# Two fp32 expert layers by seven products: block results finished inside PSUM, second products summed by DMA, units interleaved

## The chip, the cores and the metric

The kernel runs on one core of a Trainium2 chip. The time is that of one execution on the device in microseconds, from the first to the last instruction and the little around it. The engines are called PE (TensorE, the matmuls), PEld (its weight loads), DVE (VectorE), ACT (ScalarE), POOL (GpSimd) and SP (SyncE, which only starts transfers).

## The reference

```python
q_bits = (einsum('bhsd,dk->bhsk', q, proj) > 0)            # q, k, v: (2, 8, 768, 64); proj: (64, 6)
mask = q_bucket[:, :, :, None] == k_bucket[:, :, None, :]  # buckets: the six bits as a number
scores = where(mask, q @ k.T / sqrt(64), -1e9)
attn = exp(scores - max); attn = attn / (sum + 1e-9)
x = (attn @ v), heads side by side                         # (1536, 512)
h = x @ w_in; g = h - tanh(h); x = g @ w_out               # d_ff 2048
g = x @ w_gate; silu = g / (1 + exp(-g))                   # d_ff 1536
out = (silu * (x @ w_val)) @ w_out2                        # (1536, 512)
```

All of it is float32. The weights of the two expert layers arrive as 64-bit floating point numbers and are converted to float32 on the chip.

## The kernel before, in words

**Attention** runs first: 8 pairs of heads, 12 steps each (`declare_step`, L599), about 2.4 us a step. It ends near 257 us. Its transposes use both halves of the PSUM tile `t`, its second matmul the bank `x`, its hash bits the bank `h`.

**The expert layers** follow. The first product of a layer (with `w_in`, or with `w_gate` and `w_val`) is cut into units: one weight, one block of 256 columns (`i`), one block of 768 tokens (`sb`, two of them). A unit is computed as a 2 x 2 block product by seven products in place of eight (`PRODUCTS`, L736): sums and differences of the four blocks of x (made once for each token block by `x_blocks`, L332) times sums and differences of the four blocks of the weight (`declare_in`, L252). Every factor is held as a high and a low part, whose difference keeps float32's precision, so a product is two k steps of three terms: six matmuls of 128x128 by 128x384 (L769). In `products` (L741) the seven results gather in three PSUM banks: two of an `s` tile and one of `x` or `h`, by turns. Partial results are copied to SBUF on the way (`snap`, L753, ACT) and added to later ones (`add`, L756, DVE, result in SBUF). Each of the four finished 128 x 384 blocks of a unit goes through an activation: tanh on ACT and a subtraction (L721, L722), sigmoid and a multiplication (L727, L728), or the multiplication with the gate's result (L733). Then `split_g` makes its high part on ACT (L708) and its low part on POOL (L709).

**The second products** (`out_group`, L800) are groups of six matmuls (L820): 8 groups of 384 columns for a unit of layer 1, 6 of 512 columns for a pair of gate and value units. A group writes one of the two halves of `t`, and its result is added to an accumulator in SBUF by DVE (L836; for the first column block a copy by ACT or DVE, L833 and L834). At the end SP stores the accumulators in 12 transfers (L840). There are 16 units in layer 1 and 24 in layer 2, and in each the groups of an earlier unit are placed after given products (`share`, L885).

**Weights** come in chunks of 512 KB by SP (L229) and are converted by three DVE instructions (`convert`, L231, L234, L237); `declare_in` forms the block differences (L261, L264, L266) and `split_w` the parts (L243 on ACT, L245 on POOL). `declare_out` does it for the second weights (L277, L279).

**The order** of all instructions is worked out before the program is written: every operation is declared with the engines that may run it, an estimated time on each, what it reads and writes and a due time (`Plan.op`, L79); `Plan.order` (L99) plays this through, and at each moment a free engine takes the ready operation with the earliest due time. The program then issues each engine's instructions in that order. Operations marked `late` wait until attention is through, since the accumulators, the second weights and part of x's factors take over its room in SBUF (L908 to L912).

## Time and profile before

| | |
|---|---|
| median of 3 runs | 882.77 us (880.28 to 884.28) |
| the profiled execution | 878.98 us |
| its span, first to last instruction | 877.0 us |
| mean granted TensorE clock | 0.994 of full speed |

The time of the profiled execution stands for its span and 2 us around it. Busy times are read against the span; an instruction's duration is the bar that the profile draws, and the bars of successive matmuls overlap. The line numbers are those of the code above.

### The profile page before, as it was taken

Reading aid. Unit: us, or ns where it says so; the run is one execution under the profiler, and the core shown is the slowest. Engines: PE = TensorE matmul, PEld = TensorE weight load, DVE = VectorE, ACT = ScalarE, POOL = GpSimd, SP = SyncE. Lnnn points to the kernel's source line nnn. Section 1 sums busy time; section 2 is a strip of 40 time slices with the busy share of each in tenths; the row PEclk is TensorE's granted clock in tenths of the full one; section 3 lists DMA queues with packets and bytes.
Section 4 is the critical chain, followed back from the end, with each engine's and each line's share of the span. In section 5 each row is a group of like instructions: output and inputs, shape, how many; then the busy total and the mean of one; then the engine's idle time right before and its main releaser. Section 6 shows DMA issues by size and latency. Waiting matters only on the chain.

```text
span 877.0 us, 12166 instructions
## 1 busy us (share of the span) xinstructions
PE 789.9 (90%) x4332; PEld 660.4 (75%) x4332; DVE 639.1 (73%) x987; ACT 424.0 (48%) x804; POOL 529.6 (60%) x497
## 2 busy tenths in 40 slices
PE   5999999999996888988999898989989899999995
PEld 3666666666665867888889787877878888788883
DVE  6887777777858853766867779897876987877452
ACT  4787778766744533333433354444433334334220
POOL 4665677544857644665865678478585865848130
PEclk9999999999998999999999999999999999999999
DMA  8644554542111120221121210112212221210002
GB/s 214 163 121 126 128 119 116 134 89 76 55 67 49 49 72 25 73 72 49 49 88 57 72 59 14 48 38 84 96 49 85 67 89 49 72 50 23 1 37 108
DMA packets 25659, 66.46 MB, mean 76 GB/s; under 512 B 3936, under 2 KB 9312, under 8 KB 25600
## 3 DMA queue, kind: packets, MB, share of 16 engines
q1 hardware_dynamic: 25088, 64.76, 24.8%
q10 hardware_dynamic: 464, 0.80, 0.4%
q8 instruction: 34, 0.56, 0.3%
q0 software_dynamic: 48, 0.13, 0.1%
q14 instruction: 25, 0.20, 0.1%
HBM read 46.03 MB, written 3.15 MB: 56 GB/s over the span
## 4 chain that ended last, share of the span: by engine, by line
PE 68%; DVE 21%; ACT 4%; issue 3%; POOL 2%; DMA 1%; DVEq 0%; ACTq 0%
PE t L820 24%; PE s L769 20%; PE x L664 8%; PE t L640 7%; PE s L611 6%; DVE acc L836 6%; DVE m L620 2%; DVE f L234 2%; PE h L769 2%; DVE ct L756 2%; DVE acc L324 1%; ACT ct L622 1%; PE x L769 1%; DVE f L231 1%; ACT acc L833 1%
## 5 line engine op out<-in xcount | busy, mean ns | idle before, releaser
L769 PE MATMUL s<-x,wi 128*128 128x384 f32 x1200 | 241.1, 341 | 12.6 <-ACT ct L753 6.5
L769 PEld LDWEIGHTS s<-x,wi 128*128 128x128 f32 x1200 | 209.6, 188 | 28.7 <-ACT ct L753 13.7
L820 PE MATMUL t<-op,wo 128*128 128x384 f32 x768 | 157.1, 344 | 30.3 <-DVE acc L836 22.7
L820 PEld LDWEIGHTS t<-op,wo 128*128 128x128 f32 x768 | 132.6, 189 | 46.8 <-DVE acc L836 36.3
L709 POOL TENSOR_TENSOR op<-ct,op 128x384 fp32r<-128x384 f32 x112 | 125.7, 1132 | 65.3 <-ACT op L708 59.5
L836 DVE TENSOR_TENSOR acc<-t,acc 128x384 f32<-128x384 f32 (+1 forms) x172 | 101.6, 599 | 82.2 <-PE t L820 81.6
L820 PE MATMUL t<-wo,op 128*128 128x512 f32 x432 | 112.0, 399 | 15.2 <-DVE acc L836 12.3
L245 POOL TENSOR_TENSOR wi<-fs,wi 128x512 fp32r<-128x512 f32 (+1 forms) x60 | 96.9, 1619 | 34.4 <-ACT wi L243 34.3
L629 POOL TENSOR_SCALAR ct<-ct,r 128x768 f32<-128x768 f32 x96 | 94.5, 993 | 32.5 <-DVE r L628 25.8
L753 ACT ACTIVATE ct<-s 128x384 f32<-128x384 f32 x120 | 56.6, 488 | 114.8 <-PE s L769 113.2
L620 DVE TENSOR_REDUCE m<-s 128x1 f32<-128x768 f32 x96 | 89.4, 952 | 30.9 <-PE s L611 30.3
L820 PEld LDWEIGHTS t<-wo,op 128*128 128x128 f32 x432 | 77.9, 188 | 38.4 <-DVE acc L836 18.6
L622 ACT ACTIVATE ct<-s,m 128x768 f32<-128x768 f32 x96 | 85.9, 897 | 19.5 <-DVE m L620 14.9
L708 ACT ACTIVATE op<-ct 128x384 fp32r<-128x384 f32 x112 | 57.6, 522 | 77.7 <-DVE ct L733 36.3
L611 PE MATMUL s<-op 128*128 128x384 f32 x384 | 87.3, 361 | 7.9 <-ACT ct L622 7.7
L640 PEld LDWEIGHTS t<-csb,ct 128*128 128x128 f32 x576 | 63.9, 140 | 31.5 <-issue 19.9
L640 PE MATMUL t<-csb,ct 128*128 128x128 f32 x576 | 80.9, 277 | 5.2 <-POOL ct L629 2.6
L611 PEld LDWEIGHTS s<-op 128*128 128x128 f32 x384 | 65.1, 192 | 18.1 <-ACT ct L622 16.6
L756 DVE TENSOR_TENSOR ct<-s,ct 128x384 f32<-128x384 f32 x80 | 43.5, 550 | 35.0 <-PE s L769 29.6
L664 PE MATMUL x<-pt,v 128*64 128x384 f32 x384 | 69.0, 495 | 0.0
L646 ACT ACTIVATE pt<-t 128x768 f32<-128x768 f32 x58 | 47.1, 812 | 29.2 <-PE t L640 26.2
L243 ACT ACTIVATE wi<-fs 128x512 fp32r<-128x512 f32 (+1 forms) x60 | 41.8, 698 | 24.4 <-PE s L769 7.3
(110 smaller groups left out, 1076.1 us busy)
## 6 DMA issues: line engine op xcount, KB each, us to landing
raw<-in_w SPq DMA_DIRECT2D x68, 512.0 KB, 3.2
op<-q SPq DMA_DIRECT2D x84, 96.0 KB, 2.5
op<-k SPq DMA_DIRECT2D x42, 192.0 KB, 3.0
v<-in_v SPq DMA_DIRECT2D x8, 384.0 KB, 3.1
out<-acc SPq DMA_DIRECT2D x12, 256.0 KB, 2.0
y<-in_qT SPq DMA_DIRECT2D x7, 384.0 KB, 3.4
y<-in_kT SPq DMA_DIRECT2D x7, 384.0 KB, 3.9
k<-in_kT SPq DMA_DIRECT2D x4, 192.0 KB, 5.9
```

Source lines behind the costliest of these rows:

```text
L245: op({"POOL": n / 370 + 0.02}, lambda e: e.tensor_tensor(out=lo, in0=src, in1=hi.bitcast(F32), op=ALU.subtract), r=rk + [wk + (0,)], w=[wk ...
L611: g.matmul(out=s[:, kh, 0:TB], lhsT=(b, a)[first][:, q0], rhs=ks[kh][0 if first else 1], start=first, stop=not first,)
L620: op({"DVE": 0.87}, lambda g: g.tensor_reduce(out=m, in_=sv, axis=AX.XY, op=ALU.max, negate=True), r=[sk + (0,), sk + (1,)], w=[mk], due=d ...
L622: op({"ACT": 0.9}, lambda g: g.activation(out=p.rearrange("p (a b) -> p a b", a=2), in_=sv, func=ACTF.Exp, bias=m, accum_out=sm), r=[sk + ...
L629: op({"POOL": 0.95}, lambda g: g.tensor_scalar(out=p, in0=p, scalar1=r, scalar2=1.0, op0=ALU.mult, op1=ALU.mult), r=[pk, rk], w=[pk], due= ...
L640: g.transpose(out=t_t[0][:, kt // 3, c0:c0 + 128], in_=p[:, kt * 128:(kt + 1) * 128], identity=ident)
L664: g.matmul(out=x[r, :], lhsT=v[:, kt, r], rhs=pt_t[ptks[e][1]][:, kt, :], start=(kt == 0), stop=(kt == NKT - 1), tile_position=(0, 64 * e),)
L709: op({"POOL": 1.07}, lambda g: g.tensor_tensor(out=lo, in0=src, in1=hi.bitcast(F32), op=ALU.subtract), r=srck + [hk], w=[lk] + l1, due=due ...
L756: op({"DVE": 0.57}, lambda e: e.tensor_tensor(out=dst, in0=bank, in1=dst, op=ALU.add), r=[bk, dk], w=[dk], due=due)
L769: e.matmul(out=bank, lhsT=w[:, wpart, wi * 256 + k * 128:wi * 256 + k * 128 + 128], rhs=x_at(sb, xn, xpart, k), start=first and m == 0, st ...
L820: e.matmul(out=ps, lhsT=lhs, rhs=rhs, start=m == 0, stop=m == 5)
L836: op({"DVE": 0.17 + size / 960}, lambda g: g.tensor_tensor(out=acc_at(sb, j, 1, size), in0=ps, in1=acc_at(sb, j, 1, size), op=ALU.add,), r ...
```

## The change

Two of the four blocks of a unit stay in their PSUM bank: the sum, the activation's second step and both splits read and write the bank. Of the other two, one passes through SBUF as before, and one leaves PSUM with the activation's second step, as all blocks of a gate unit do. One of the seven products and all groups of second products share a ring of four banks (both halves of `t`, `x`, `h`). A group's result is copied by ACT or DVE into a staging buffer in SBUF (except for the first and last column block of layer 1); when three or four stand there, POOL starts a transfer that adds them, in layer 1 to the accumulator in SBUF, in layer 2 to the output in HBM. The products of two successive units are issued by turns, and the groups are spread evenly between them. Weights are laid out in the order in which the products use them, and converted earlier. The tiles of attention's loads share room with `raw`, `fs` and `f`, and the second weights have room of their own. The planner's estimates are changed, and it does not let two operations marked with `port` run on DVE and POOL at one time. The diff, cut to its core:

```diff
-WN = {n: i for i, n in enumerate(("B11", "B21", "B22", "T1", "T3", "T2", "T4"))}
+WN = {n: i for i, n in enumerate(("B11", "T1", "B21", "T2", "B22", "T3", "T4"))}
...
+        eng = {e: t * (1 if e == "PE" or not self.n_first else self.SAFE) for e, t in eng.items()}
+        self.ops.append((eng, fn, deps, due, self.LAT if lat is None else lat, late, after,
+                         DUE["alt"] if alt is None else alt, port))
...
+                held_back = []
+                while q and (q[0][1] in started or e in ops[q[0][1]][8] and port > now + 1e-9):
+                    held_back.append(heapq.heappop(q))
+                n = heapq.heappop(q)[1] if q else None
+                for h in held_back:
+                    if h[1] not in started:
+                        heapq.heappush(q, h)
+                if n is None:
+                    continue
...
-    raw_t = tiles(ctx, "raw", 2, [128, 512], I64)
-    fs = tiles(ctx, "fs", 1, [128, 8 * 256])[0]
-    f_t = tiles(ctx, "f", 1, [128, 512])[0]
+    used = set()
+
+    raw_a = tiles(ctx, "raw", 1, [128, 2048])[0]
+    raw_t = [raw_a[:, 1024 * i:1024 * i + 1024].bitcast(I64) for i in range(2)]
+    ldk_t = [raw_a[:, 1024 * i:1024 * i + S] for i in range(2)]
+    fs = tiles(ctx, "fs", 1, [128, 7 * 256])[0]
+    y_t = [fs[:, 0:2 * S].rearrange("p (i s) -> p i s", i=2)]
+    pw = fs[:, 2 * S:].bitcast(BF16).rearrange("p (j c) -> p j c", j=4)
+    f_a = tiles(ctx, "f", 1, [128, S])[0]
+    f_t = f_a[:, 0:512]
+    wo_t = tiles(ctx, "wo", NWO, [128, 2, 512], F32R)
+    before = {("fs", k): [("y", 0)] if k < 3 else [("y", 1)] if k < 6 else ["pw"] for k in range(7)}
+    before.update({("raw", i): [("ldk", i, h) for h in range(2)] for i in range(2)})
+    before["f", 0] = [("ldq", 0, h) for h in range(2)]
+
+    def first(keys):
+        new = [k for k in keys if k not in used]
+        used.update(new)
+        return list(keys) + [j for k in new for j in before[k]]
...
-    W_TS, W_STT = 0.82, 1.05
-
-    def convert(c, dst, dk, due, after):
+    W_TS, W_STT = 0.43, 0.69
+    WALT, LEAD, OLEAD = 3.0, 16, 14
+    BOTH = ("POOL", "DVE")
...
+        for j, (lo, hi) in enumerate(((0, 2), (3, 4))):
+            convert(c + j, pair(lo, hi), [("fs", lo), ("fs", hi)], due - LEAD + 2 * j, after, 2)
+
+        def sub(dst, a, b, n, due):
+            op({"POOL": pool(256 * n), "DVE": dve(256 * n)}, lambda e: e.tensor_tensor(
+                out=pair(*dst), in0=pair(*a), in1=pair(*b), op=ALU.subtract,
+            ) if n == 2 else e.tensor_tensor(out=blk(dst[0]), in0=blk(a[0]), in1=blk(b[0]), op=ALU.subtract),
+               r=[("fs", k) for k in sorted({*a, *b})], w=first([("fs", k) for k in dst]), due=due, alt=WALT, port=BOTH)
+
+        sub((1, 5), (3, 4), (0, 3), 2, due - LEAD + 4)
+        sub((3,), (4,), (1,), 1, due - LEAD + 5)
+        sub((6,), (2,), (3,), 1, due - LEAD + 5.5)
+        for part, lo, n, d in (("a", 0, 3, 8), ("b", 3, 2, 5), ("c", 5, 2, 2)):
...
+        convert(order_c[name, f], f_t, [("f", 0)], due - OLEAD, after)
+        hi, lo = wo_t[wk[1]][:, 0, :], wo_t[wk[1]][:, 1, :]
+        op({"ACT": 0.63}, lambda e: e.activation(out=hi, in_=f_t, func=ACTF.Copy),
+           r=[("f", 0)], w=[wk + (0,)], due=due - 6)
+        op({"POOL": pool(512), "DVE": dve(512)}, lambda e: e.tensor_tensor(
+            out=lo, in0=f_t, in1=hi.bitcast(F32), op=ALU.subtract,
+        ), r=[("f", 0), wk + (0,)], w=[wk + (1,)], due=due - 5.5, alt=WALT, port=BOTH)
...
+    T1_AT, T2_AT = [6, 7, 16], list(range(8, 16)) + [6, 7, 16]
+
+    def t_slot(layer):
+        if layer == 1:
+            i, k, w = slot("tt", len(T1_AT), T1_AT, ct_first)
+        else:
+            i, k, w = slot("t2", len(T2_AT), T2_AT, lambda i: [("st", 1, (i - 8) // 4, (i - 8) % 4)] if 8 <= i < 16 else [("tt", T1_AT.index(i))])
...
+            if layer == 1:
+                first = [("xf", r, m)]
+            else:
+                first = [("acc", r // 2, 4 * (r % 2) + k) for k in range(m * DM // TB, ((m + 1) * DM - 1) // TB + 1)]
+        if layer == 1:
+            at_ = lambda n=1: ct_a[:, (8 + 4 * r + m) * TB:(8 + 4 * r + m + n) * TB]
+        else:
+            at_ = lambda n=1: late["acc"][r // 2][:, (r % 2) * 1536 + m * DM:(r % 2) * 1536 + (m + n) * DM]
+        return at_, key, first
...
+    EARLY, XDUE, EALT, ZDUE = 14, 13, 1.0, (0, 10)
+
+    def tt(dst, dk, a, ak, b, bk, alu, due, port):
+        op({"DVE": dve(TB), "POOL": pool(TB)} if port else {"DVE": 0.56}, lambda e: e.tensor_tensor(out=dst, in0=a, in1=b, op=alu),
+           r=[ak, bk], w=dk, due=due, alt=ALT, port=BOTH * port)
+
+    def split_g(key, src, sk, due, psum):
         (hi, hk, h1), (lo, lk, l1) = g_slot(), g_slot()
-        op({"ACT": 0.5}, lambda g: g.activation(out=hi, in_=src, func=ACTF.Copy), r=srck, w=[hk] + h1, due=due)
-        op({"POOL": 1.07}, lambda g: g.tensor_tensor(out=lo, in0=src, in1=hi.bitcast(F32), op=ALU.subtract),
-           r=srck + [hk], w=[lk] + l1, due=due + 0.6)
+        op({"ACT": 0.52}, lambda g: g.activation(out=hi, in_=src, func=ACTF.Copy), r=[sk], w=[hk] + h1, due=due)
+        tt(lo, [lk] + l1, src, sk, hi.bitcast(F32), hk, ALU.subtract, due + 0.6, not psum)
...
+    def block_tanh(key, src, sk, due, psum, keep, spare=None):
+        t, tk, t1 = spare or t_slot(1)
+        op({"ACT": 0.51}, lambda e: e.activation(out=t, in_=src, func=ACTF.Tanh), r=[sk], w=[tk] + t1, due=due)
+        d, dk = (src, sk) if keep else (t, tk)
+        tt(d, [dk], src, sk, t, tk, ALU.subtract, due + 0.6, not psum)
+        split_g(key, d, dk, due + 1.2, keep and psum)
...
+    RING = [(("t", 0), t_t[0][:, 0, :]), (("t", 1), t_t[0][:, 1, :]), (("x", 0), x_t[0]), (("h", 0), h_t[0])]
+
+    def bank_slot():
+        return RING[ring("bank", len(RING))[1]]
...
-        banks = [s_t[z][:, 0, 0:TB], (x_t, h_t)[z][0][:, 0:TB], s_t[z][:, 1, 0:TB]]
-        bkeys = [("s", z, 0), ((("x", 0), ("h", 0))[z]), ("s", z, 1)]
+        bkeys = [("s", z, 0), None, ("s", z, 1)]
+        banks = [s_t[z][:, 0, 0:TB], None, s_t[z][:, 1, 0:TB]]
...
-                add(c0, k0, bank, bk, e)
-                block((layer, i, sb, 0, 0), c0, [k0], e + 1)
+                add(bank, bk, bank, bk, c0, k0, e)
+                block((layer, i, sb, 0, 0), bank, bk, e + 0.6, True, True, (c0, k0, []))
             elif n == 3:
                 snap(c2, [k2] + f2, bank, bk, e - 1)
             elif n == 4:
-                add(c2, k2, bank, bk, e)
-                block((layer, i, sb, 0, 1), c2, [k2], e + 1)
+                add(bank, bk, bank, bk, c2, k2, e)
+                block((layer, i, sb, 0, 1), bank, bk, e + 0.6, True, True, (c2, k2, []))
             elif n == 5:
-                add(c1, k1, bank, bk, e - 1)
-                block((layer, i, sb, 1, 1), c1, [k1], e + 1)
+                add(c1, k1, bank, bk, c1, k1, e - 1)
+                block((layer, i, sb, 1, 1), c1, k1, e + 1, False, False)
             else:
-                block((layer, i, sb, 1, 0), bank, [bk], e)
-            between(n)
-
-    def acc_at(sb, j, n=1, size=TB):
-        return late["acc"][sb][:, j * size:(j + n) * size]
+                block((layer, i, sb, 1, 0), bank, bk, e, True, False)
+
+        return product
...
+        k, ps = bank_slot()
+        ps = ps[:, 0:size]
...
+        aks = [("acc", sb, n * t + c) for c in range(n)]
+        if layer == 1 and i in (0, NP1 - 1):
+            if i == 0:
+                op({"DVE": dve(TB), "ACT": 0.5}, lambda g:
+                   g.activation(out=acc_at(sb, j), in_=ps, func=ACTF.Copy) if g is nc.scalar else
+                   g.tensor_copy(acc_at(sb, j), ps), r=[k], w=[("acc", sb, j)], due=e, late=True)
+            else:
+                op({"DVE": 0.57}, lambda g: g.tensor_tensor(
+                    out=acc_at(sb, j), in0=ps, in1=acc_at(sb, j), op=ALU.add,
+                ), r=[k, ("acc", sb, j)], w=[("acc", sb, j)], due=e, late=True)
...
+            at_, key, first = stage(layer, m)
+            op({"ACT": 0.18 + size / 1200, "DVE": dve(size)}, lambda g, at_=at_:
+               g.activation(out=at_(), in_=ps, func=ACTF.Copy) if g is nc.scalar else g.tensor_copy(at_(), ps),
+               r=[k], w=[key] + first, due=e, late=layer == 2, alt=EALT)
+            if m == 0:
+                stages[layer, "at"] = at_
+            if m == n - 1:
+                at_ = stages[layer, "at"]
+                keys = [key[:3] + (c,) for c in range(n)]
+                if layer == 1:
+                    op({"POOL": 1.0}, lambda g, at_=at_: g.dma_start(out=acc_at(sb, 4 * t, 4), in_=at_(4), accum_op=ALU.add),
+                       r=keys + aks, w=aks, due=e + 1, lat=5.0, late=True)
+                else:
+                    o = out[sb * S + t * TB:sb * S + t * TB + TB, :].rearrange("(j p) c -> p j c", p=128)
+                    src = lambda at_: at_(3).rearrange("p (j c) -> p j c", j=3)
+                    ok = ("o", sb, t)
+                    if i == 0:
+                        op({"SP": 0.5}, lambda g, at_=at_: g.dma_start(out=o, in_=src(at_)), r=keys, w=[ok], due=e + 1, lat=4.0)
+                    else:
+                        op({"POOL": 1.0}, lambda g, at_=at_: g.dma_start(out=o, in_=src(at_), accum_op=ALU.add),
+                           r=keys + [ok], w=[ok], due=e + 1, lat=5.0)
...
+    slots, start = [], 0
+    for n, u in enumerate(units):
+        slots += [(start + 2 * m, n, m) for m in range(7)]
+        start += 14 if n + 1 < len(units) and u[0] == "in" != units[n + 1][0] else 7
+    outs, credit, run = [], 0.0, {}
+    for _, n, m in sorted(slots):
+        name, i, sb = units[n]
+        if m == 0:
+            run[n] = products(name, i, sb)
+        run[n](m)
+        if m == 6:
+            if name == "in":
+                outs += [(1, i, sb, j) for j in range(8)]
+            elif name == "val":
+                outs += [(2, i, sb, j) for j in range(6)]
+        credit += (8 / 7, 3 / 7)[n >= 20] if outs else 0
+        flush = m == 6 and name == "in" != units[n + 1][0]
+        while outs and (credit >= 1 or flush):
+            credit -= 1
             out_group(*outs.pop(0))
-        if name == "in":
-            outs += [(1, i, sb, j) for j in range(8)]
-        elif name == "val":
-            outs += [(2, i, sb, j) for j in range(6)]
+        credit = max(credit, 0)
```

## Rows read from the trace of the kernel before

**Rows 1.** The page's engine totals: busy us (share of the span), instructions.

```profile
PE 789.9 (90%) x4332; PEld 660.4 (75%) x4332; DVE 639.1 (73%) x987; ACT 424.0 (48%) x804; POOL 529.6 (60%) x497
```

**Rows 2.** Stages: length, busy us (instructions) of PE, PEld, DVE, ACT, POOL, clock, DMA.

```profile
257.00:340.00 83.00, 66.48 (x331) 57.92 (x330) 52.58 (x70) 34.97 (x69) 44.68 (x33) 0.96 0.14 45
340.00:500.00 160.00, 144.89 (x793) 136.37 (x792) 113.06 (x178) 61.98 (x120) 102.72 (x87) 1.00 0.19 65
500.00:592.00 92.00, 80.22 (x426) 74.40 (x425) 79.30 (x104) 42.81 (x77) 62.03 (x42) 0.98 0.13 41
592.00:855.00 263.00, 248.57 (x1243) 218.45 (x1242) 192.18 (x270) 98.35 (x194) 161.73 (x128) 1.00 0.17 59
855.00:877.00 22.00, 12.62 (x48) 8.16 (x46) 6.00 (x9) 0.53 (x1) 1.47 (x2) 1.00 0.29 107
```

**Rows 3.** One of these stages, PE and PEld alone: L769, then L820.

```profile
592.00:855.00 263.00, 162.81 (x858) 149.51 (x858) 1.00 0.17 59
...
592.00:855.00 263.00, 98.95 (x385) 69.19 (x384) 1.00 0.17 59
```

**Rows 4.** The chain that ended last: start us, us, what (merged matmuls).

```profile
604.39 4.18 PE s L769 x24
...
655.86 2.73 PE t L820 x12
```

**Rows 5.** PE's waits from 257 to 592: us in total, times, longest.

```profile
PE t L820 <- DVE acc L836: 22.7, 28, 3.2
...
PE h L769 <- DVE op L319: 4.2, 1, 4.2
...
PE s L769 <- POOL wi L245: 0.5, 1, 0.5
```

**Rows 6.** PE's waits from 592 to 873.

```profile
PE t L820 <- DVE acc L836: 12.3, 16, 1.8
```

**Rows 7.** Timeline of PE: start, us, instruction [idle before <- releaser].

```profile
322.19 1.31 PE L820 MATMUL t<-op,wo 128*128 128x384 f32 x6 [0.58 <-ACT acc L833]
...
868.30 1.67 PE L820 MATMUL t<-wo,op 128*128 128x512 f32 x6 [0.79 <-DVE acc L836]
```

**Rows 8.** DVE groups from 340 to 500: busy us, mean ns | idle before.

```profile
L836 DVE TENSOR_TENSOR acc<-t,acc 128x384 f32<-128x384 f32 x71 | 38.7, 553 | 33.6 <-PE t L820 33.5
...
L722 DVE TENSOR_TENSOR ct<-ct 128x384 f32<-128x384 f32 x11 | 10.1, 918 | 0.0
...
L722 DVE TENSOR_TENSOR ct<-s,ct 128x384 f32<-128x384 f32 x9 | 4.9, 548 | 0.5 <-ACT ct L721 0.5
```

**Rows 9.** Groups of POOL and ACT over the whole span.

```profile
L709 POOL TENSOR_TENSOR op<-ct,op 128x384 fp32r<-128x384 f32 x112 | 125.7, 1132 | 65.3 <-ACT op L708 59.5 <-PE t L820 4.7 <-PE s L769 1.1
...
L721 ACT ACTIVATE ct<-s 128x384 f32<-128x384 f32 x16 | 7.8, 486 | 9.1 <-PE s L769 7.7 <-POOL x L319 1.4
```

**Rows 10.** A group of POOL; DMA issues: count, KB each, median us to landing.

```profile
L850 POOL DMA_DIRECT2D csb<-in_cst x1 | 0.7, 734 | 0.4 <-issue 0.4
...
raw<-in_w SPq DMA_DIRECT2D x68, 512.0 KB, 3.2
...
out<-acc SPq DMA_DIRECT2D x12, 256.0 KB, 2.0
...
csb<-in_cst POOLq DMA_DIRECT2D x1, 131.0 KB, 4.6
```

**Rows 11.** Timeline at the end of the span, DVE.

```profile
872.45 1.29 DVE L836 TENSOR_TENSOR acc<-t,acc 128x512 f32<-128x512 f32 x2 [1.75 <-PE t L820]
```

**Rows 12.** Tiles y and pw (durations ns, first and last start); timelines of DVE, PE.

```profile
L578 PE MATMUL h<-y,pj x56: 486/498/510, 21.1 to 188.4; 128*32 128x384 f32 x56
...
L465 PEld LDWEIGHTS <-pw x36: 95/97/147, 6.5 to 204.6; 128*128 128x128 bf16 x36
...
217.99 0.41 DVE L231 TENSOR_SCALAR fs<-raw 128x512 uint32<-128x512 uint32 x1
...
251.01 0.87 PE L640 MATMUL t<-csb,ct 128*128 128x128 f32 x6
```

More of the change, by code (lines that the diff above doesn't have):

```diff
@@ L77, in __init__, with op @@
         self.n_first = 0
[L79 removed]
+    def op(self, eng, fn, r=(), w=(), due=0.0, lat=None, late=False, after=0.0, alt=None, port=()):
         n = len(self.ops)
@@ L153, in order @@
                 end = now + o[0][e]
+                if e in o[8]:
+                    port = end
                 free[e] = end
@@ L753, in snap, with add, product @@
             op({"ACT": 0.49}, lambda e: e.activation(out=dst, in_=bank, func=ACTF.Copy), r=[bk], w=dk, due=due)
-        def add(dst, dk, bank, bk, due):
-            op({"DVE": 0.57}, lambda e: e.tensor_tensor(out=dst, in0=bank, in1=dst, op=ALU.add), r=[bk, dk], w=[dk], due=due)
-        for n, (xn, wn, bi, first) in enumerate(PRODUCTS):
+        def add(dst, dk, bank, bk, c, ck, due):
+            op({"DVE": 0.56}, lambda e: e.tensor_tensor(out=dst, in0=bank, in1=c, op=ALU.add), r=[bk, ck], w=[dk], due=due)
+        def product(n):
+            xn, wn, bi, first = PRODUCTS[n]
+            if bi == 1:
+                bkeys[1], b = bank_slot()
+                banks[1] = b[:, 0:TB]
             bank, bk = banks[bi], bkeys[bi]
@@ L823, in out_group @@
+                    e.matmul(out=ps, lhsT=lhs, rhs=rhs, start=c == 0, stop=c == 5)
+                    c += 1
         op({"PE": dur}, mm, r=[wk + (h,) for wk in wks for h in range(2)] + [g for gg in gs for g in gg[2]], w=[k],
-           due=d, lat=0.25, late=True)
+           due=d, lat=0.25)
         e = clock[0]
-        if layer == 1:
-            size, ak, first = TB, [("acc", sb, j)], []
-        else:
-            size, ak = DM, [("acc2", sb, j)]
-            first = [("acc", sb, m) for m in range(j * DM // TB, ((j + 1) * DM - 1) // TB + 1)]
@@ L831, in out_group @@
-        if i == 0:
-            op({"DVE": 0.15 + size / 960, "ACT": 0.17 + size / 1175}, lambda g:
-               g.activation(out=acc_at(sb, j, 1, size), in_=ps, func=ACTF.Copy) if g is nc.scalar else
-               g.tensor_copy(acc_at(sb, j, 1, size), ps), r=[k], w=ak + first, due=e, late=True)
-        else:
-            op({"DVE": 0.17 + size / 960}, lambda g: g.tensor_tensor(
-                out=acc_at(sb, j, 1, size), in0=ps, in1=acc_at(sb, j, 1, size), op=ALU.add,
-            ), r=[k] + ak, w=ak, due=e, late=True)
```

155 lines of the change are left out of this document (62 added, 93 removed).

## The prediction, made before the change was run

> **What bounds the kernel now.** I read the page's engine totals first. TensorE (PE) is busy for 789.9 of 877.0 us, DVE for 639.1, POOL for 529.6, ACT for 424.0 [rows 1]. That 90% flatters PE: rows of back-to-back matmuls show 24 of 384 columns in 4.18 us, so one goes out every 0.174 us, and 12 of 512 columns in 2.73 us, one every 0.2275 us [rows 4]. So I counted matmuls by stage [rows 2, 3] and multiplied by these two prices. Attention keeps PE full until about 257 us. After that:
> 257 to 340: 331 x 0.174 = 57.6 of 83 us, 25.4 lost. 340 to 500: 793 x 0.174 = 138.0 of 160, 22.0 lost. 500 to 592: 426 x 0.174 = 74.1 of 92, 17.9 lost. 592 to 855: 858 x 0.174 + 385 x 0.2275 = 236.9 of 263, 26.1 lost. From 855 to the last matmul's end at 872.4: 48 x 0.2275 = 10.9 of 17.4, 6.5 lost. Together 97.9 us in which no matmul is issued. This, not PE's work, is what a change of this kind can touch; the matmuls themselves are not altered.
>
> The waits name what PE waits for. In both layers the first place is the second-product group (L820) waiting for the add into the accumulator (L836): 22.7 us in layer 1 and the change of layers, 12.3 us in layer 2 [rows 5, 6]. The waits understate it, since a busy bar covers the pipeline's tail: where group follows group, each takes 0.58 us idle plus 1.31 us of bar in layer 1 and 0.79 plus 1.67 in layer 2 [rows 7], starts 1.9 and 2.46 us apart, though six matmuls need 1.04 and 1.36. Two banks (`t`) alternate, and a third group may start only when the first has been added. It is the same when ACT empties the bank (the 0.58 us row), so the engine isn't the cause: two banks are too few for a round trip through an engine that also has weights to convert. The other waits are the change of token block (one of 4.2 us on L319 [rows 5]) and the snapshots between products of one unit.
>
> **The change part by part.**
> *Four banks in place of two, copies in place of adds, interleaved units.* The groups get the ring t0, t1, x, h, shared with one of the seven products. In layer 1 a unit is 7 products and 8 groups, 15 x 1.04 = 15.7 us, and takes 9 ring slots: a bank comes round after 4 x 1.74 = 7.0 us, where now it is 3.9. A group holds its bank for its matmuls and one copy of about 0.49 us (the tanh that reads PSUM takes 486 ns [rows 9]), on ACT or DVE. The kept block holds it for add, tanh, subtraction and two splits, 1.04 + 5 x 0.55 = 3.8 us plus hand-overs: less than 7.0 as well. With units two abreast, a bank that is continued after a snapshot gets one more product between. I take back 18 of the 22.0 us of 340 to 500 and 17 of the 26.1 of 592 to 855 (layer 2 has half a group for each product, so less of its wait is groups), and 5.5 of 6.5 at the end, where groups stand alone. At the two changes of block the x sums and splits stay one chain, and only the groups that queue there are freed: 12 of 25.4, and 7 of 17.9. Sum: 59.5 us. Lower bound 30 (ring freed, but copies late), upper 79 (half of the rest too).
>
> *Load of the engines.* 340 to 500 is 793 / 90 = 8.8 units. ACT does 62.0 / 8.8 = 7.0 us a unit [rows 2] and gets 8 copies, 3.9: 10.9 of 15.7. DVE does 12.8, loses 8 adds of 553 ns (4.4) [rows 8], gets two low splits of PSUM-held blocks (1.1) and the share of block operations that POOL takes today: about 10. POOL does 11.7, loses those two splits of 1132 ns [rows 9], gets two DMA issues of 734 ns [rows 10]: about 11. All below PE's 15.7, so I charge nothing. The cover is PE itself; should one of them run late by its whole slack, it is the rival on copies below. A DVE operation with both inputs in SBUF takes 918 ns, with one in PSUM 548 [rows 8]: moving three of four blocks there helps DVE, beside PE. SP only loses: 12 stores at the end against 4 in the middle. Writing PSUM from DVE has no row; I take 0.55 us, bounds 0.45 (nothing gained by the write) and 0.92 (the worst two-input row), 5 operations a unit, at worst 1.9 us of DVE, still in its slack.
>
> *Sums by DMA.* Layer 1: six of eight column blocks, two token blocks, two transfers each: 24. Layer 2: 20, and 4 plain stores. Each moves 768 KB. From 256 KB in 2.0 us and 512 KB in 3.2 [rows 10], 768 KB would land in 4.4 us; with the destination read as well, twice the bytes, 0.8 + 2 x 3.6 = 8.0. The far end is the only POOL-issued transfer, 131 KB in 4.6 us [rows 10], at whose pace it would be 27 us; that one ran in the crowded first microseconds. What it must fit: two staging sets in layer 1, groups 1.95 us apart, so from the fourth copy to the copy that reuses the set 5 x 1.95 - 0.49 = 9.3 us. The POOL issue (0.7) and a POOL operation ahead of it (1.1) included, the plain transfer needs 6.2 and hides; the doubled needs 9.8, 0.5 too many, 24 times: 12 us. Behind such a late transfer ACT stands, and with it the snapshots and the tanh. I take 4, between 0 and 12 nearer to the rows of like size; the far end, (0.7 + 27 + 1.1 - 9.3) x 24, some 470 us, I hold for unlikely. In layer 2 four sets turn over in about 45 us: nothing, at either end. On POOL the issue waits for four copies with weight splits queued behind it; they have the lead of 16 us for that.
> The Trainium skill (Collectives: The Full Stack, section The bandwidth ceiling: the fold count and why AG ≠ RS ≠ AR) states a rule that speaks against this change: a reducing transfer reads two sources for one write, and so runs at about half the rate of a copy. No run here shows it yet; by it the price would be the 12 us of the doubled reading and not 4.
>
> *The end.* Today the last add ends at 873.7 [rows 11], 1.3 us behind the last matmul, and the span ends 3.3 us later. Then: copy 0.65, issue 0.7, landing 4.4 to 8.0, which is 1.2 to 4.8 us more than today's 4.6; I take 3 (far end 24).
>
> *Shared tiles.* `fs`, `raw` and `f` take over the room of `y`, `pw`, `ldk`, `ldq`. The last reads of `y` are at 188.4 and of `pw` at 204.6 us, the first conversion starts at 217.99 [rows 12]: 0, while the conversions stay behind 208 us; if the last reads were late by over 10 us, the first products would be. But the ring takes t0 and t1 before attention is through: its last transposes start at 251.01 and need both [rows 12]. A kept block there delays a transpose by up to 4 us, for two units: 0 to 8, I take 2. Earlier weights, their new order and the planner's port rule: 0, since PE waits 0.5 us for them today [rows 5].
>
> Sum: 59.5 - 4 - 3 - 2 = 50.5 us off the profiled execution's 879.0 gives 828.5. The median of the runs, 882.8, stands 3.8 above it, so I forecast 832.
>
> **The rivals.**
> *Doubled reading:* as above, 8 us more, 840. For it: the sum can't be made without the old value. Against: nothing in the trace.
> *Copies are late:* ACT's queue takes the place of DVE's, the snapshots stand behind copies, half of the 59.5 stays: 862. For it: the 0.58 us wait is ACT's already [rows 7]. Against: four banks and two engines to copy with.
> *The chains at the changes of block shorten too,* because groups no longer wait for attention's end: half of the other 38 us, 813. For it: the 4.2 us wait is one DVE operation [rows 5].
> *The waits only change their names* (banks held by blocks instead of by adds): 883.
> *The accumulating transfer overruns its window* (the slower side): its place is the reuse of a layer-1 staging set, 24 times. Each microsecond beyond 9.3 costs 24; the gain is used up at 9.3 + 54.5 / 24 = 11.6 us from copy to landing. At 12.5 us it is 3.2 x 24 = 77 in place of 4: 905. For it: the POOL-issued row's pace [rows 10]. Against: that row's bytes ran beside all the first loads.
>
> **How the numbers follow.** Forecast 0.42, doubled reading 0.14, late copies 0.18, shorter chains 0.05, names only 0.05, overrun 0.16. The likeliest case's own range is 808 to 856. To hold 8 in 10 the range runs from 803 (bounds of the shorter chains) to 884 (late copies and names only): 0.42 + 0.14 + 0.18 + 0.05 and part of 0.05. Faster by over 0.5%, about the smallest difference that a measurement of this kernel can tell from none: 0.42 + 0.14 + 0.18 + 0.05 = 0.79. Within it: 0.05. Slower: 0.16.
>
> **What would show it.** Right: between 340 and 500 us about 100 matmuls in each 18 us; L820's waits on its bank below 8 us in all; landing of the accumulating transfers at 4.4 to 8 us; DVE down by some 50 us, ACT up by some 70. Wrong: ACT's or DVE's copies waiting for a DMA (overrun), PE's waits moved to the s banks or to copies (names, late copies), transposes waiting for a block before 257 us, a last landing over 10 us behind the last matmul.

## The result, and the profile after

The changed kernel takes 821.86 us (median of 4 runs, 820.66 to 823.82) beside 882.1 us for the kernel before (4 runs, 880.28 to 884.28): a ratio of 0.932 with a 95% interval of 0.929 to 0.935. That is 60.2 us less. The forecast was 832 us, the range 803 to 884. The profiled execution took 823.82 us, its span 822.0 us (before: 878.98 and 877.0): 55.2 us less, where 50.5 was forecast. The other 5 us are the place of the two profiled executions among their runs: 3.1 us below the median before, 2.0 above it after. In the changed kernel L850 is the product matmul, L904 the group's, L830 the snapshot, L833 the add of a snapshot, L779 every other two-input operation on a block (subtraction, multiplication, low split), L784 the high split, L923 a group's copy, L931 and L940 the adding transfers of layer 1 and of layer 2.

The page's engine totals, busy us (share of the span) and instructions:

```profile
PE 766.3 (93%) x4332; PEld 662.5 (81%) x4332; DVE 579.8 (71%) x1031; ACT 470.7 (57%) x912; POOL 363.7 (44%) x389
```

Against [rows 1] DVE lost 59 us and ACT gained 47, as meant (50 and 70 were named); POOL lost 166, which the prediction had not seen: the low splits, on POOL alone before (125.7 us in [rows 9]), now run on DVE or POOL, and 24.9 us of them are left on POOL.

The stage windows, with the columns of [rows 2]; then PE and PEld alone in one of them, for L850 and for L904:

```profile
257.00:340.00 83.00, 81.12 (x455) 76.30 (x452) 61.25 (x111) 48.06 (x100) 26.93 (x24) 1.00 0.38 98
...
340.00:500.00 160.00, 157.27 (x894) 154.47 (x893) 113.28 (x204) 88.39 (x183) 69.78 (x63) 1.00 0.65 151
500.00:565.00 65.00, 58.79 (x303) 53.75 (x302) 52.05 (x86) 32.23 (x61) 28.05 (x22) 0.97 0.35 100
565.00:780.00 215.00, 214.02 (x1115) 197.28 (x1114) 149.06 (x268) 108.51 (x211) 83.80 (x71) 1.00 0.58 126
780.00:804.00 24.00, 19.81 (x90) 16.21 (x89) 4.38 (x8) 8.66 (x17) 3.81 (x4) 1.00 0.64 95
804.00:822.00 18.00, 0.00 (x0) 0.00 (x0) 0.00 (x0) 0.00 (x0) 2.58 (x2) 0.52 0.62 92
...
565.00:780.00 215.00, 149.53 (x798) 139.68 (x798) 1.00 0.58 126
...
565.00:780.00 215.00, 81.53 (x317) 58.35 (x316) 1.00 0.58 126
```

Counted with the prices of [rows 4], the time without a matmul is now 83 - 455 x 0.174 = 3.8 us from 257 to 340; 160 - 894 x 0.174 = 4.4 to 500; 65 - (257 x 0.174 + 46 x 0.2275) = 9.8 at the change of layers (46 of its 303 matmuls are of groups with 512 columns); 215 - (798 x 0.174 + 317 x 0.2275) = 4.0 in layer 2 to 780; and 1.4 to the last matmul's end at 800.9 (18 product and 72 group matmuls). Together 23.4 us, where it was 97.9. PE's waits say the same. The two longest from 257 to 565, then the one longest from there on (us in total, times, longest):

```profile
PE s L850 <- DVE s L779: 2.1, 2, 1.5
PE s L850 <- ACT ct L830: 2.0, 3, 1.0
...
PE s L850 <- ACT op L784: 1.1, 1, 1.1
```

The group's wait for its bank, 22.7 and 12.3 us in [rows 5, 6], is gone from the head of the list; from 257 to 565 us L904 waits 1.0 us for an add of the last column block (L917) and 0.8 us for copies.

But in the last window of the stages no engine computes for 18 us: the kernel ends in transfers. The timeline of POOL from 789 us on (start, us, instruction [idle before <- releaser]) and the last copy on ACT:

```profile
789.81 1.30 POOL L940 DMA_DIRECT2D out<-acc  x1 [1.97 <-ACT acc L923]
797.59 1.28 POOL L940 DMA_DIRECT2D out<-acc  x1 [6.48 <-issue]
805.48 1.29 POOL L940 DMA_DIRECT2D out<-acc  x1 [6.62 <-issue]
813.09 1.29 POOL L940 DMA_DIRECT2D out<-acc  x1 [6.33 <-issue]
...
800.96 0.60 ACT L923 ACTIVATE acc<-h 128x512 f32<-128x512 f32 x1 [0.76 <-PE h L904]
```

All copies are done at 801.56, yet the last transfer is issued 11.5 us later. The program has no wait among these four, which add to different rows of the output, and the profile puts the 6.3 to 6.6 us before each of the last three down to "issue". The landings in the trace, at 797.3, 805.2 and 812.8 us, are each 0.3 us before the next issue: POOL itself starts one only when the one before has landed. The span ends 21.1 us behind the last matmul, where it was 4.6.

The transfers by tile (count, KB each, median us to landing):

```profile
acc<-ct POOLq DMA_DIRECT2D x24, 768.0 KB, 6.7
out<-acc POOLq DMA_DIRECT2D x20, 768.0 KB, 7.7
...
out<-acc SPq DMA_DIRECT2D x4, 768.0 KB, 4.0
```

### The profile page after: what moved, and what is told of

The parts are those of the page before. It is cut to its first block, busy times and chain, and to the rows that moved or that the text cites. A ratio compares the mean times of both kernels' runs of the same rounds, so it can differ in the third digit from the quotient of the medians.

```text
span 822.0 us, 12296 instructions
## 1 busy us (share of the span) xinstructions
PE 766.3 (93%) x4332; PEld 662.5 (81%) x4332; DVE 579.8 (71%) x1031; ACT 470.7 (57%) x912; POOL 363.7 (44%) x389
## 4 chain that ended last, share of the span: by engine, by line
PE 54%; DVE 8%; issue 5%; POOL 1%; ACT 1%; DMA 1%; POOLq 0%; DVEq 0%; ACTq 0%
PE s L850 25%; PE t L904 13%; PE h L904 6%; PE x L904 3%; PE x L850 3%; PE t L850 1%; DVE op L779 1%; DVE x L363 1%; DMA raw<-in_w 1%; DVE f L276 1%; PE h L850 1%; POOL out L940 1%; DVE ct L779 1%; PE x L706 1%; DVE f L279 0%
## 5 line engine op out<-in xcount | busy, mean ns | idle before, releaser
L850 PE MATMUL s<-x,wi 128*128 128x384 f32 x1200 | 235.9, 338 | 7.9 <-DVE s L779 2.1
L850 PEld LDWEIGHTS s<-x,wi 128*128 128x128 f32 x1200 | 209.7, 188 | 18.6 <-ACT op L784 3.5
L664 ACT ACTIVATE ct<-s,m 128x768 f32<-128x768 f32 x96 | 85.8, 896 | 21.1 <-DVE m L662 17.1
L830 ACT ACTIVATE ct<-s 128x384 f32<-128x384 f32 x120 | 58.4, 491 | 64.3 <-PE s L850 63.7
L904 PE MATMUL t<-op,wo 128*128 128x384 f32 x372 | 74.5, 337 | 2.4 <-DVE acc L917 1.0
L904 PE MATMUL t<-wo,op 128*128 128x512 f32 x270 | 69.1, 393 | 0.0
L904 PEld LDWEIGHTS t<-op,wo 128*128 128x128 f32 x372 | 64.9, 188 | 4.9 <-ACT ct L923 1.5
L287 POOL TENSOR_TENSOR wi<-fs,wi 128x512 fp32r<-128x512 f32 (+1 forms) x39 | 59.7, 1551 | 20.3 <-ACT wi L285 19.8
L904 PEld LDWEIGHTS t<-wo,op 128*128 128x128 f32 x270 | 50.1, 188 | 8.4
L779 POOL TENSOR_TENSOR ct<-ct 128x384 f32<-128x384 f32 x24 | 24.7, 1028 | 61.8 <-ACT ct L791 30.0
L850 PE MATMUL s<-op,wi 128*128 128x384 f32 x240 | 48.6, 337 | 2.1 <-DVE ct L779 1.0
L779 POOL TENSOR_TENSOR op<-ct,op 128x384 fp32r<-128x384 f32 x24 | 24.9, 1038 | 55.4 <-ACT op L784 48.6
L940 POOL DMA_DIRECT2D out<-acc x20 | 26.2, 1310 | 49.3 <-issue 19.7
L706 PEld LDWEIGHTS x<-pt,v 128*64 128x64 f32 x384 | 24.7, 136 | 28.5 <-issue 28.5
```

What stands on the lines that cost most here:

```text
L287: op({"POOL": pool(n), "DVE": dve(n)}, lambda e: e.tensor_tensor(out=lo, in0=src, in1=hi.bitcast(F32), op=ALU.subtract), r=rk + [wk + (0,) ...
L664: op({"ACT": 0.9}, lambda g: g.activation(out=p.rearrange("p (a b) -> p a b", a=2), in_=sv, func=ACTF.Exp, bias=m, accum_out=sm), r=[sk + ...
L706: g.matmul(out=x[r, :], lhsT=v[:, kt, r], rhs=pt_t[ptks[e][1]][:, kt, :], start=(kt == 0), stop=(kt == NKT - 1), tile_position=(0, 64 * e),)
L779: op({"DVE": dve(TB), "POOL": pool(TB)} if port else {"DVE": 0.56}, lambda e: e.tensor_tensor(out=dst, in0=a, in1=b, op=alu), r=[ak, bk], ...
L830: op({"ACT": 0.49}, lambda e: e.activation(out=dst, in_=bank, func=ACTF.Copy), r=[bk], w=dk, due=due)
L850: e.matmul(out=bank, lhsT=w[:, wpart, wi * 256 + k * 128:wi * 256 + k * 128 + 128], rhs=x_at(sb, xn, xpart, k), start=first and m == 0, st ...
```

## The experiments

Runs of the kernel before beside them took 879.6 to 881.3 us (medians). A single run can be off by some 2 us, as the four of the changed kernel show; where only one was made, it is said.

### What the ring and the order bring

The kernel before with the ring alone, adds still on DVE:

```diff
-        banks = [s_t[z][:, 0, 0:TB], (x_t, h_t)[z][0][:, 0:TB], s_t[z][:, 1, 0:TB]]
+        banks = [s_t[z][:, 0, 0:TB], None, s_t[z][:, 1, 0:TB]]
...
+            if bi == 1:
+                bkeys[1], b = bank_slot()
+                banks[1] = b[:, 0:TB]
...
-        k = ring("t", 2)
+        k, ps = bank_slot()
```

> Kernel before (882 us) with one part of the change alone: groups and the middle product share the ring t0, t1, x, h. Theory (two banks were the main cause): the waits of L820's groups on the adds, 35 us in PE's rows, fall by two thirds, 850 to 865 us. Rival (DVE's queue was the cause, more banks only fill up behind it): above 872 us.

840.88 us (one run), 39 less than the run of before beside it (880.26), and better than was expected. Its longest waits of PE from 257 to 855 us:

```profile
PE s L777 <- DVE ct L761: 12.9, 10, 3.5
PE s L777 <- ACT ct L758: 8.7, 15, 0.8
PE t L828 <- DVE acc L844: 5.2, 4, 1.6
```

The group's wait for its add (here L828 on L844) fell to 5.2 us with the adds where they were. Two banks were too few; the adding engine was not the cause. Now the products wait, for snapshots (L758) and their adds (L761).

The same with the units issued by turns as well:

```diff
-        products(name, i, sb, between)
+        slots += [(start + 2 * m, n, m) for m in range(7)]
...
+        run[n](m)
```

> Kernel before with the ring of four (840.9 us) and the products of two units by turns, groups spread evenly; activations, splits, sums, weights and planner as before. Theory (ring and interleaving are nearly the whole gain; the rest unloads engines that are not full): 818 to 828 us. Rival (with POOL and DVE as full as before, interleaving can't pay; the moved work is needed too): 834 us or above.

824.96 us (one run): 16 more. Its last matmul ends at about 819.3 of a span of 823.2 us.

Now the same two parts, each taken out of the changed kernel alone. A ring of two:

```diff
-        return RING[ring("bank", len(RING))[1]]
+        return RING[ring("bank", 2)[1]]
...
-                bkeys[1], b = bank_slot()
+                bkeys[1], b = RING[2 + z]
```

> Changed kernel (821.9 us), but the groups of second products get only t0 and t1 and the product takes x or h by turns, as before; everything else as changed. Theory (two banks were too few): groups wait for their bank again, 835 to 850 us, L904's waits on the copies above 12 us in all. Rival (even spacing of the groups and copies on a freer engine did it): a copy comes back within 1.9 us, well inside the 3.9 us in which two banks come round, and the time stays below 828 us.

848.04 us (one run), 26 more. PE's longest waits from 257 to 855 us show the group's bank again, held by copies now in place of adds:

```profile
PE t L904 <- ACT acc L923: 8.2, 12, 0.7
PE t L904 <- DVE ct L923: 3.6, 4, 2.2
PE t L904 <- ACT ct L923: 2.8, 7, 0.6
```

Units one after the other:

```diff
-        slots += [(start + 2 * m, n, m) for m in range(7)]
-        start += 14 if n + 1 < len(units) and u[0] == "in" != units[n + 1][0] else 7
+        slots += [(start + m, n, m) for m in range(7)]
+        start += 7
```

> Changed kernel, but the products of a unit follow each other without those of the next unit between. Theory (interleaving pays for the waits on snapshots): PE waits for ACT's snapshots and for blocks in the s banks again, 835 to 850 us. Rival (the ring of four alone did it): below 828 us.

855.61 us (one run), 34 more, above the expected range; the direction was right. The longest waits, same stretch:

```profile
PE s L850 <- ACT ct L830: 11.6, 19, 1.2
PE s L850 <- DVE op L779: 7.5, 10, 1.2
PE s L850 <- DVE s L779: 5.3, 6, 1.2
PE s L850 <- DVE ct L779: 4.2, 4, 1.1
```

These are the chains within a unit. Interleaving is worth twice here what it is in the kernel before (34 and 16 us). I put that down to the blocks kept in PSUM, whose bank is held through add, activation and splits; no run shows it apart.

### What the planner's rule brings

Rule off and estimates as before:

```diff
-                         DUE["alt"] if alt is None else alt, port))
+                         DUE["alt"] if alt is None else alt, ()))
...
-    W_TS, W_STT = 0.43, 0.69
+    W_TS, W_STT = 0.82, 1.05
```

> Changed kernel, but the planner lets marked operations run on DVE and POOL at one time and counts the conversions at the old 0.82 and 1.05 us. Theory (an order detail, PE barely waits for weights): 818 to 828 us. Rival (the conversions' place in the queues is part of the gain): 832 us or above.

842.19 us (839.83 to 843.34, 4 runs), ratio 0.956 [0.954, 0.958]: 20 more than the changed kernel. The theory fell, the rival held. The last matmul ends at about 820.0 us, where ring and interleaving alone put it at 819.3. So all else that the change moves (kept blocks, sums by DMA, earlier weights) shortened the computing by nothing on balance until the planner's part was there. On balance only: against ring and interleaving it issues 43 matmuls more from 257 to 340 us (437, not 394) and 36 fewer from 340 to 500 (860, not 896). Which of its two halves? The rule alone off, new estimates kept (the first hunk above):

> Changed kernel (821.9 us) with the new estimates of 0.43 and 0.69 us for the conversions, but the planner lets marked operations run on DVE and POOL at one time. With the old estimates as well it took 842.2. If the rule makes the difference (with it the order has no two SBUF operations at one time, and the estimates come true), 834 to 845 us. Rival (the estimates alone matter: long conversions in the plan push the additions back), 820 to 828 us.

852.59 us (849.26 to 853.85, 4 runs), ratio 0.970 [0.968, 0.972], 31 more than the changed kernel and above the theory's range. Two groups of DVE from 340 to 500 us (busy us, mean ns | idle before), with both inputs in SBUF, first without the rule:

```profile
L779 DVE TENSOR_TENSOR op<-ct,op 128x384 fp32r<-128x384 f32 x8 | 10.6, 1327 | 0.0
L279 DVE SCALAR_TENSOR_TENSOR fs<-raw,fs 128x512 uint32<-128x512 uint32 x11 | 10.0, 906 | 0.0
```

and in the changed kernel:

```profile
L779 DVE TENSOR_TENSOR op<-ct,op 128x384 fp32r<-128x384 f32 x11 | 8.2, 741 | 0.0
...
L279 DVE SCALAR_TENSOR_TENSOR fs<-raw,fs 128x512 uint32<-128x512 uint32 x10 | 6.8, 684 | 0.1
```

On the mean an operation takes up to 1.8 times as long where the order lets POOL run beside it. The trace of the kernel before shows the same from instruction to instruction: after 257 us its block operations with both inputs in SBUF (`ct<-ct`) took 550 ns where POOL computed nothing beside them (24 of them) and 1242 ns where it did (39); those with one input in PSUM (`ct<-s,ct`) took 551 and 550. The Trainium skill (SBUF — State Buffer, section Who interferes with whom) says that a DVE instruction with two SBUF inputs contends with a GpSimd instruction that reads SBUF, and that one with at most one SBUF input does not, outside DVE's two-port modes. The trace agrees with the first, and with the second for the block operations: the L779 groups that read PSUM stay at 0.55 to 0.57 us in either kernel. The first instruction of a conversion, with one SBUF input (L231), did suffer in the kernel before: 0.42 us alone, 0.81 and 0.96 on the mean beside POOL. Whether it runs in such a mode no run shows; the rule covers it too. PE's two longest waits from 257 to 855 us without the rule:

```profile
PE s L850 <- ACT ct L830: 7.9, 3, 4.1
PE s L850 <- DVE s L779: 7.5, 6, 3.2
```

Few and long, which fits chains that now and then meet a POOL operation that makes them late. Why the new estimates without the rule are 10 us worse than the old ones wasn't tried; I would say that estimates which hold only with the rule make a tighter plan that breaks more often.

### What the sums by DMA cost

All sums by DVE again, from PSUM into the accumulator, in the changed kernel (with the stores by SP at the end):

```diff
-        if layer == 1 and i in (0, NP1 - 1):
+        if True:
...
-                op({"DVE": 0.57}, lambda g: g.tensor_tensor(
-                    out=acc_at(sb, j), in0=ps, in1=acc_at(sb, j), op=ALU.add,
+                op({"DVE": 0.17 + size / 960}, lambda g: g.tensor_tensor(
+                    out=acc_at(sb, j, 1, size), in0=ps, in1=acc_at(sb, j, 1, size), op=ALU.add,
```

> Changed kernel, but no transfers that add: DVE adds each group to an accumulator in SBUF, and SP stores 12 blocks at the end, as before. Theory (banks and interleaving did it; the transfers only unload DVE): the end gets some 15 us shorter, DVE rises to about 13 of 15.7 us a unit and still fits, 806 to 822 us. Rival (the adds on DVE were the cause): PE waits for DVE again, above 840 us.

817.68 us (one run): 4 less than the changed kernel. The last add on DVE (start, us, instruction [idle before]):

```profile
811.68 0.69 DVE L922 TENSOR_TENSOR acc<-h,acc 128x512 f32<-128x512 f32 x1 [0.67 <-PE h L904]
```

It ends at 812.4, and the span at 815.8. The computing is 10.7 us longer than with the transfers (the last matmul ends at about 811.6, not 800.9), the end 16.9 us shorter (4.2 us behind the last matmul, not 21.1). The sums by DMA relieve DVE (609.0 us busy here, 579.8 there) and lose more at the end.

Did the transfers cost anything in their window? One staging set in layer 1 in place of two:

```diff
-            stages[layer] = ring(("st", layer), (2, 4)[layer - 1])[1]
+            stages[layer] = ring(("st", layer), (1, 4)[layer - 1])[1]
```

> Changed kernel with one staging set in place of two in layer 1: the next copy follows the fourth one 1.95 us later, so the transfer (0.87 us issue, 6.7 us to landing) has 1.5 us instead of 9.3 and overruns it by 6.1 us, 24 times. Theory (a late transfer stands in the copies' queue and stops PE after the free banks are used up, about 5 us): 24 x 1 to 24 x 6 us more, 846 to 960 us. Rival (four banks and the order worked out around it hide it): below 835 us.

854.27 us (one run), 32 more, at the lower end of the theory's range. The copies wait for landings:

```profile
DVE ct L923 <- DMA acc<-ct: 9.4, 8, 2.2
ACT ct L923 <- DMA acc<-ct: 7.7, 8, 1.6
```

From 362 to 479 us a transfer is issued every 9.65 us (13 of them, 362.41 to 478.21), with two sets every 8.0 (15, 362.56 to 474.64): 1.65 us more each, and 24 x 1.65 = 40 us is near the 32 lost. With one set the groups bunch behind each landing while products go on, which is why it doesn't cost the whole landing. In the changed kernel the same view has one such wait of 1.5 us in the whole program: two sets hide the transfer.

### The end

One transfer for each group in layer 2, 256 KB of 128 rows in place of 768 KB of 384:

```diff
-            if m == n - 1:
+            if layer == 2:
+                o = out[sb * S + j * 128:sb * S + j * 128 + 128, :]
...
+                    op({"POOL": 0.9}, lambda g, at_=at_: g.dma_start(out=o, in_=at_(), accum_op=ALU.add),
+                       r=[key, ok], w=[ok], due=e + 1, lat=5.0)
+            elif m == n - 1:
```

> Changed kernel, but in layer 2 each group's 256 KB are added to the output by a transfer of their own, three times as many. It tells why the last four transfers of the changed kernel are issued 7.6 to 7.9 us apart, each just when the one before has landed. Theory (the descriptors of one 768 KB accumulating transfer fill the room there is for them, 1024 bytes a partition, so POOL can't write the next): three small ones fit, the last are issued as their copies end, last landing 5 to 9 us behind the last copy, 807 to 813 us. Rival (POOL waits for every accumulating transfer before the next, whatever its size): nine of them in a row at 4 us or more behind the last groups, 825 us or above.

808.55 us (one run), span 806.8. POOL's last issues, then the landing:

```profile
796.79 0.86 POOL L933 DMA_DIRECT2D out<-acc  x1 [1.02 <-ACT acc L923]
798.73 0.88 POOL L933 DMA_DIRECT2D out<-acc  x1 [1.08 <-issue]
800.09 0.87 POOL L933 DMA_DIRECT2D out<-acc  x1 [0.47 <-issue]
...
out<-acc POOLq DMA_DIRECT2D x60, 256.0 KB, 4.3
```

Issued 1.4 to 1.9 us apart with 4.3 us to landing, up to three are in flight at a time. So adding transfers need not follow each other, and it isn't the rate of the bytes: 256 KB each 1.65 us (the three above) is 1.6 times the rate of 768 KB each 7.8 us. It can be the rows in flight, 3 x 128 here and 1 x 384 there, or the bytes in flight, 768 KB in both. In layer 1 of the changed kernel two 768 KB transfers of 128 rows go out 2.4 us apart, less than one landing of 6.7 us:

```profile
446.33 0.84 POOL L931 DMA_DIRECT2D acc<-ct  x1
448.76 1.18 POOL L931 DMA_DIRECT2D acc<-ct  x1 [1.59 <-ACT op L784]
```

There 1536 KB are in flight in 256 rows, which speaks for the rows; but these transfers add in SBUF and not in HBM. That the room for a transfer's list of rows is what runs out fits this and the issue times (0.88 us for 128 rows, 1.31 for 384), but it is argued: giving it more room wasn't tried.

The end without adding transfers: the last column block's sums are fetched back early, added by DVE and stored by SP:

```diff
+        elif layer == 2 and i == NP2 - 1:
+            at_, key, first = stage(layer, m)
...
+            op({"DVE": 0.17 + size / 960}, lambda g: g.tensor_tensor(out=at_(), in0=ps, in1=at_(), op=ALU.add),
+               r=[k, key], w=[key], due=e, late=True)
+            op({"SP": 0.5}, lambda g: g.dma_start(out=out[sb * S + j * 128:sb * S + j * 128 + 128, :], in_=at_()),
+               r=[key], w=[("oo", sb, j)], due=e, late=True)
```

> Changed kernel, but for the last column block of layer 2 the sum so far is loaded back from the output into the staging set by SP, DVE adds each group to it, and SP stores each 256 KB as before the change. Theory (the end costs 16 us more than before, all of it transfers): last matmul near 801 us as in the changed kernel, end 4 to 5 us behind it, 805 to 809 us. Rival (the loads or the adds delay the last products, or the rest of the gain hangs on copies there): 815 us or above.

805.75 us (803.29 to 806.54, 5 runs), ratio 0.914 [0.912, 0.916]; the last add starts at 799.23 and takes 0.69, the span ends at 803.1. The end is worth 16 us.

### The splits

The two kept blocks leave PSUM with the activation's second step, so their splits read SBUF:

```diff
-                block((layer, i, sb, 0, 0), bank, bk, e + 0.6, True, True, (c0, k0, []))
+                block((layer, i, sb, 0, 0), bank, bk, e + 0.6, True, False, (c0, k0, []))
...
-                block((layer, i, sb, 0, 1), bank, bk, e + 0.6, True, True, (c2, k2, []))
+                block((layer, i, sb, 0, 1), bank, bk, e + 0.6, True, False, (c2, k2, []))
```

> Changed kernel, but the two kept blocks leave PSUM with the activation's second step, and both splits read SBUF. Theory (the splits in PSUM only move work of POOL to DVE and hold the bank longer; no engine is full): 818 to 826 us. Rival (it is the missing collisions of DVE and POOL in SBUF that pay): 832 us or above.

818.32 us (817.81 to 819.51, 4 runs), ratio 0.929 [0.927, 0.931], 3.5 less than the changed kernel: holding the banks through the splits costs a little and brings nothing. What exactly the 3.5 us are (banks free earlier, or splits that POOL may take too) wasn't separated.

Both repairs together (the two diffs above):

> The two experiments that were faster than the changed kernel (821.9 us) in one: last column block of layer 2 added by DVE and stored by SP (805.8 alone), and both splits of the kept blocks read SBUF (818.3 alone). If both gains are of their own kind, 16 and 3.5 us, 800 to 804 us. Rival (the 3.5 us are an accident of the worked-out order): 804.5 us or above.

803.26 us (802.32 to 803.37, 5 runs), ratio 0.912 [0.910, 0.913]: the best of all, 18.6 us below the changed kernel and 2.5 below the one with the end alone repaired.

## Why the prediction was right, and where its terms were off

The forecast, 50.5 us off the profiled execution, came out at 55.2, by errors that partly cancel. Its terms beside what the windows show, in us:

| term | forecast | measured |
|---|---|---|
| 257 to 340 | 12 | 21.6 (25.4 to 3.8) |
| 340 to 500 | 18 | 17.6 (22.0 to 4.4) |
| change of layers | 7 | 8.1 (17.9 to 9.8) |
| layer 2, up to the end groups | 17 | 22.1 (26.1 to 4.0) |
| end groups | 5.5 | 5.1 (6.5 to 1.4) |
| DMA window | -4 | one wait of 1.5, within the rows above |
| end | -3 | -16.5 (4.6 to 21.1) |
| transposes | -2 | -2.1 (12 fewer product matmuls before 257) |
| sum | 50.5 | 55.9 (span: 55.0) |

The two changes of block and layer 2 gave 15.8 us more than was said, the end took 13.5 more and the DMA window 4 less. That these nearly cancel is luck; the ring and the order of the units are not.

**The ring and the order of the units** were rightly named: 39 us and 16 in the kernel before, with the sums left on DVE. "The engine isn't the cause" held, and 340 to 500 came out as costed: the ring alone has 888 matmuls there, where the kernel before has 793 and the changed one 894. **The load of the engines** could be charged nothing, as said, though it fell out otherwise: at 894 / 90 = 9.9 units in that window ACT does 8.9 us a unit (10.9 was said), DVE 11.4 (10) and POOL 7.0 (11). **The transposes** came out in size and not in mechanism: none of their waits is put down to a block's instruction.

**"Earlier weights, their new order and the planner's port rule: 0, since PE waits 0.5 us for them today"** is the step that failed, in both halves. That wait is one for the first weights (L245). PE from 257 to 340 us (length, busy us (matmuls), clock, DMA), in the kernel before with ring and interleaving, then in the changed kernel without the rule, with the new estimates and with the old:

```profile
257.00:340.00 83.00, 73.78 (x394) 0.92 0.15 51
...
257.00:340.00 83.00, 72.92 (x387) 0.96 0.30 80
...
257.00:340.00 83.00, 78.03 (x437) 1.00 0.36 93
```

The changed kernel has 455 there. Ring and interleaving bring 394 - 331 = 63 matmuls against [rows 2], 63 x 0.174 = 11.0 us: the 12 of the forecast. The other 61, 10.6 us, lie before 300 us: from 257 to 300 the changed kernel issues 227, ring and interleaving 164, the kernel before 163. There the change has a part that the prediction charged nothing. In the kernel before, the second weights wait for attention's room in SBUF. The low half that the first group of second products still needs is formed by 276.1 us (L279), and the group follows; in the changed kernel the weights have room of their own, are formed from 247.3 us on (L322), and groups fill the gap behind attention. The first group before, and in the changed kernel:

```profile
277.19 2.25 PE L820 MATMUL t<-op,wo 128*128 128x384 f32 x12
...
265.19 1.33 PE L904 MATMUL h<-op,wo 128*128 128x384 f32 x6
```

From 250 to 282 us the groups issue 18 matmuls in the kernel before, 1 and 0 in its two variants, and 42 to 50 in the changed kernel and in all ten made from it, the rule on or off. With the rule off PE still issues 194 (new estimates) and 211 (old) from 257 to 300 us, so 30 to 47 of the matmuls gained there come without the rule. That the second weights bring them is read from these traces; they weren't moved alone. No list of waits shows it, since the order worked out beforehand simply puts the groups later.

The rule's own half is spread over the program: with it off the changed kernel loses 30.7 us, and the last matmul ends at 827.0 us in place of 800.9. PE issues 68 matmuls fewer from 257 to 340 us, 24 fewer from 340 to 500 and 35 fewer from 565 to 780. The rule acts on the conversions and on the two-input operations of blocks and x that read SBUF alone, not only on what PE was seen to wait for. The price of 918 ns in [rows 8], which I read as a cost of SBUF inputs, was a cost of POOL beside them: in the changed kernel's groups of DVE over the whole span the same operation takes 551 ns.

```profile
L779 DVE TENSOR_TENSOR ct<-ct 128x384 f32<-128x384 f32 x16 | 8.8, 551 | 0.7 <-ACT ct L798 0.6
```

So an operation out of SBUF costs no more than one out of PSUM (0.55 us) as long as POOL stays away.

**The rival of the shorter chains** had its reason right in part: groups no longer wait for attention's end. At the two changes of block 29.7 us came back, 10.7 more than the forecast had; this rival had 19 more.

**The end** is the term that was mis-sized: 3 was said, 16.5 measured. From the last matmul to the end of the span it is 0.7 us to the end of the last copy, 11.5 until its transfer is issued, 7.7 from there to landing and 1.2 after it. Copy and landing lie within what was said; the issue took 1.3, where 0.7 was said, and a landing is counted from the start of its issue. Without the 11.5 the end would be 5.0 us longer than before, near the 4.8 of the upper bound. That four transfers would stand in line behind one another was not thought of: the sum took one transfer where the last column block has four.

**The DMA window**: the landing of 6.7 us lies nearer to the doubled reading (8.0) than to the plain one (4.4). It is 1.7 times the 4.0 of the plain stores to HBM, and the 7.7 of the adding transfers to HBM 1.9 times. So the trace agrees in direction with the rule that the prediction cited from the Trainium skill (Collectives: The Full Stack, section The bandwidth ceiling: the fold count and why AG ≠ RS ≠ AR); the page gives it for the reducing step between cores, not for a transfer within one. SP issued the plain stores and POOL the adding ones, and no run parts the issuer from the adding. But 6.7 us from the issue's start to landing, and a POOL operation of some 1 us ahead of it, fit the window of 9.3, so neither the 4 us nor the 12 were paid, and the overrun stayed away. Late copies did not come: ACT and DVE had slack.

The ladder as the runs show it: 882.1 before; 840.9 with the ring; 825.0 with the units by turns; 817.7 with all else but the DMA sums; 821.9 as changed, the computing 10.7 us shorter and the end 16.9 longer; 805.8 with the end repaired; 803.3 with the splits from SBUF. Whether the rule would help the kernel before on its own wasn't tried.

## What to carry to other kernels

Price a matmul from back-to-back rows, each width by its own price, count matmuls by stage, and look at what is missing; where it goes to a bank's round trip, more banks help before a faster engine does. A rule that keeps two engines from running certain operations at one time isn't free of effect because nobody waits for those operations: compare the durations of the same operation in different company. Where the order is worked out beforehand, a late operand shows as no wait at all: ask when each is first ready. Cost the last transfers of a kernel as a queue, not one by one.

## What the runs showed that was not expected

- Adding transfers of 768 KB in 384 rows, issued by POOL, follow each other 7.6 to 7.9 us apart though none waits for another in the program; of 128 rows they overlap (256 KB 1.4 us apart, in layer 1 768 KB once 2.4).
- An adding transfer of 768 KB lands in 6.7 us in SBUF and 7.7 in HBM; a plain one by SP in 4.0.
- A DVE operation that reads a PSUM bank and writes back into it takes hardly longer than one into SBUF: 0.565 us for `s<-s,ct`, 0.552 for `ct<-s,ct`, at 128x384 (L833).
- The same low split with both inputs in SBUF took 1327 ns on DVE where POOL ran freely, 741 under the rule, and 592 from 340 to 500 us with the splits from SBUF (26 of them).
